# Attention and MLP block on one core: other orders for the tiles of two steps of a unit, and matmul waits on TensorE's own semaphore

## The chip, the core and the metric

The kernel runs on one core of a Trainium2 chip. The core has a matrix engine (TensorE, in the profile PE, with its weight loads as PEld), VectorE (DVE), ScalarE (ACT), GpSimd (POOL) and SyncE (SP, which issues most DMAs). Each engine works through its own queue in order; engines wait for one another by semaphores. The metric is the device time of one execution in microseconds, lower is better. Matmul results go to PSUM, of which the kernel uses eight banks of 128 x 512 float32, and from which VectorE and ScalarE read them.

## What is computed

`x` has 2048 rows of 512. After a layer norm, two branches read it: an attention block with 32 heads of 16, and an MLP of width 1376 whose output goes through a SiLU. The result is `x + s * g`.

```python
x = A_x
xn = _layernorm(x, axis=-1)
qkv = (xn @ wqkv).reshape(B, S, 3, H, Dh).transpose(2, 0, 3, 1, 4)
q, k, v = qkv[0], qkv[1], qkv[2]
p = softmax(einsum("bhqd,bhkd->bhqk", q, k) * Dh ** -0.5)
s = einsum("bhqk,bhkd->bhqd", p, v).transpose(0, 2, 1, 3).reshape(B, S, D) @ wo
h = gelu(xn @ w1 + b1)
g = silu(h @ w2 + b2)
return x + s * g
```

## The kernel before

**Stages.** Layer norm and the first projections come first (0 to 52 us), then the *dense stage* (52 to 474 us) with the remaining projections and the MLP, then the *attention stage* (to 1492 us), then the output projection of the tokens, which ends the kernel. Operands of the dense products are split into a high and a low part, so that each product is three matmuls (high by high, high by low, low by high).

**Dense stage and its row halves.** In the dense stage TensorE's array is used as two halves of 64 rows, a = 0 and a = 1, which work at the same time. `run` (L614) takes two lists of matmuls, one for each half, and issues them in turn; `fill` (L563) puts matmuls of the attention scores between them. A sum over 512 inputs is thus made partly on one half and partly on the other, in the same PSUM bank. Where a half goes on with a sum that the other half wrote last, that earlier write must be over. `mm` (L583) keeps the books for this: `writer` has the half and the number of the last matmul on each sum, and `prog["seen"]` the number of the newest matmul that is known to be over. Where the number is newer, the matmul waits for a marker. `mark` (L600) makes one: a copy of one element into `junk`, on ScalarE (or VectorE) that waits for the newest matmul so far; the later matmul then waits for the copy. Markers are put into the work ahead of need, by `down` (L645, after the fourth pair of matmuls, or two on VectorE in the last but one call) and `quad` (L702). There are 92 on ScalarE and two on VectorE. Matmuls of scores move `prog["seen"]` on as well, since they wait for VectorE, which waited for earlier ones (`taken`, L577).

**Attention stage.** A unit is four heads and 512 queries (`NU` = 32 units); a unit has 16 steps, one for each block of 128 keys. Step n belongs to unit `ua` and has the number `ka` in it, `divmod(n, 16)`. A step is written out as a string of letters (`ORDER`, L40, worked through at L970):

- T (`t_one`, L732): the scores of one head with the keys on the partitions, 128 x 512, into one of four banks; ScalarE takes the exponential from there (L741). The first two T of a step use half a = 1 of the array, the last two a = 0.
- S, X, Y (`s_op`, L209): the scores of a later unit with the queries on the partitions, needed for the maximum of the softmax; VectorE reduces each tile of 512 columns to its maximum (L189). An S is a whole tile: the first of a step uses half a = 0, the second a = 1. X and Y together are one tile: X its first 256 columns on half 0, Y its other 256 on half 1, in one bank; ahead of Y a NOP on TensorE waits until X is over (L225). One reduction follows Y.
- V (`pv_step`, L798): the exponentials of the step before times the values, for four heads, on the whole array, summed over a unit's 16 steps in one bank. When the last is done, which is the V in step ka = 0 of the next unit, VectorE copies the sum to SBUF (L811, `os`). The next unit's first V, in step ka = 1, needs that bank.

The S, X and Y tiles take turns in three banks. `s_ring` (L90) is the queue of these: S takes the oldest and puts it back at the end at once, X takes the oldest and Y puts it back. With the usual order of a step, the first S takes the bank of the last step's first S, X that of the second S, and the second S that of the halved tile. Each must wait until VectorE has reduced what is in its bank.

The string `TSXTTSTYV` is used in nearly all steps up to n = 491, where the maxima of all units are done; from there it is `TTTTV`, with the output projection between. Other work is hung on steps with `at` (L919): after the T with the index `pos`, by default the last. In step ka = 2 these are the loads of a later unit's queries (`load_qt`, six DMAs on SP's queue) and, in four units, a GpSimd subtraction for the output weights (`wo_low`).

Of the kernel before, what the change touches and what calls it, by code (L numbers as in the profile page):

```python
# [8 lines left out]
F32 = mybir.dt.float32  # L9
F32R = mybir.dt.float32r  # L10
AF = mybir.ActivationFunctionType
# [26 lines left out]
HB = 4  # L38
W2B = 2
ORDER = {0: "TTTTV", 3: "TSXTTSTYV"}  # L40
HC = CH // 2
PAIRED = 28
KB = 3
# [5 lines left out]
def fused(ctx: ExitStack, tc: tile.TileContext, x, wqk, wv, wo, w1, b1, w2, b2, out):  # L49
    nc = tc.nc  # L50
# [17 lines left out]
    ident_r = keep.tile([P, P], F32R, name="ident_r")  # L68
# [17 lines left out]
    SYNC = mybir.DependencyInfo(mybir.DependencyClass.Sync, mybir.DependencyReason.DATA)  # L86
# [5 lines left out]
    def s_tile(held=False):  # L92
        pool = s_ring.pop(0)
        if not held:
            s_ring.append(pool)
        return pool.tile([P, CH], F32, name="ps"), pool
# [58 lines left out]
    done = {u: 0 for u in range(NU)}  # L155
# [16 lines left out]
    def at_of(job):  # L172
        u, st, p = job
        return divmod(st, NCH) if u % (NCH * KB) else divmod(st, NCH)[::-1]

    def s_mm(ps, job, a, c0, k0, w):
        u, st, p = job
        qi, ki = at_of(job)
        if u not in MX:
            MX[u] = qring.tile([P, GH, NCH, NCH, 2], F32, name="mx")  # L180
        r = slice(64 * a, 64 * a + 3 * DH)
        k0 += ki * CH
        return nc.tensor.matmul(ps[:, c0:c0 + w], QS[u][r, p, qi * P:(qi + 1) * P],  # L183
                                kts[u // NCH % KB][p][r, k0:k0 + w], start=True, stop=True).ins

    def s_max(ps, job, heads, parts):
        u, p = job[0], job[2]
        qi, ki = at_of(job)
        nc.vector.tensor_reduce(MX[u][:, 2 * p:2 * p + 2, qi, ki][:, heads, parts], ps.rearrange("p (n c) -> p n c", c=HC), axis=AX.X, op=OP.max)  # L189
        done[u] += 1  # L190
        if ended:
            s_end0(ended.pop())
        if done[u] == 64:
            ended.append(u)
        if done[NU - 1] == 64:
            s_end0(ended.pop())
# [12 lines left out]
    def s_op(op):  # L209
# [6 lines left out]
        elif op == "X":  # L216
            if not cut:
                cut[:] = [jobs.pop(0), 0]
            ps, pool = s_tile(True)
            x = s_mm(ps, cut[0], 0, 0, cut[1] * HC, HC)  # L220
            cut[2:] = [ps, pool, x]
            run_off()
        else:
            job, n, ps, pool, x = cut
            hold = nc.tensor.nop().ins  # L225
            tc.add_manual_dep(hold, x.name, SYNC, reason="row tile done")
            s_mm(ps, job, 1, HC, n * HC, HC)
            s_max(ps, job, slice(0, 2), n)
# [33 lines left out]
    prog = {}  # L262
# [42 lines left out]
    for i in range(nu):  # L305
        pairs.append(ms[2 * i:2 * i + 2])
        if (i + 1) * len(qs) // nu > i * len(qs) // nu:
            g, c = qs[i * len(qs) // nu]
            pairs.append([("q", g, c), ("q", g, c + 1)])
    parts = [(c, f, h) for c in range(NCH) for f in range(FT) for h in range(2)]  # L310
    is_m = [pair[0][0] == "m" for pair in pairs]
    plan, nd = [("first", g, i) for g in range(VQ - 1) for i in (0, 2)], 0
    for j in range(len(pairs)):
        for h in range(2):
# [9 lines left out]
            n = 2 if nd < len(parts) and parts[nd][2] and ready - nd > room else 1  # L324
            n = max(n, need - 2 * (left - 1))
            while nd < ready and n > 0:
                c, f, k = parts[nd]
# [25 lines left out]
    def w2_load(i):  # L353
        if i < len(ms):
            W2[ms[i][1:]] = w_new(w2[ms[i][2]], 2, "raw2")

    def w2_split(i):
        if i < len(ms):
            W2[ms[i][1:]] = w_split(W2[ms[i][1:]], "w2", W2B)
# [178 lines left out]
    keep_r = ctx.enter_context(tc.tile_pool(name="keep_r", bufs=1, side="right"))  # L538
# [19 lines left out]
    writer = {}  # L558
    s_when, put, row = [], [0], [0, 0]
# [22 lines left out]

    def mm(a, key, ps, lhs, rhs, first, last):  # L583
        r = slice(64 * a, 64 * a + 64)
        token = None
        if not first and writer[key][0] != a and writer[key][1] > prog["seen"]:
            if not tokens or tokens[-1][0] < writer[key][1]:
                mark()
            prog["seen"], token = next(x for x in tokens if x[0] >= writer[key][1])
        i = nc.tensor.matmul(ps, lhs[r], rhs[r], start=first, stop=last).ins  # L590
        if token is not None:
            tc.add_manual_dep(i, token, SYNC, reason="other row tile")
        prog["pe"] += 1
        row[a] += 1
        latest[0] = (prog["pe"], i.name)
        writer[key] = (a, prog["pe"])

    tokens, latest = [], [None]

    def mark(dve=False):  # L600
        if dve:
            i = nc.vector.tensor_copy(junk[:, 1:], ident_r[:1, :1].bitcast(F32)).ins
        else:
            i = nc.scalar.activation(junk[:, :1], ident_r[:1, :1].bitcast(F32), AF.Copy).ins  # L604
        tc.add_manual_dep(i, latest[0][1], SYNC, reason="row tile done")
        tokens.append((latest[0][0], i.name))

    def mark_early(n):
        if prog["seen"] < n:
            mark()  # L610

    junk = keep_r.tile([1, 2], F32, name="junk")

    def run(ops, hooks={}):  # L614
        for n, two in enumerate(zip(*ops)):
            prog["n"] += 1
            for a in range(2):
                fill(a)
                mm(a, *two[a])
            for h in hooks.get(n, []):  # L620
                h()
# [23 lines left out]
    def down(c, f, part):  # L645
        i = c * FT + f
        if f == 0 and part == 0:
            PA[c] = [ps_v.tile([P, D], F32, name="pv")] + [ps_t.tile([P, D], F32, name="pst") for t in range(3)]
        h, w = HS[c, f], W2[c, f]
        side = (part + i) % 2  # L650
        ops = [[], []]
        for a in range(2):
            for t in ((0, 1), (2, 3))[(a + side) % 2]:
                ts = slice(t * P, (t + 1) * P)
                for n, (x, y) in enumerate(((0, 0), (0, 1), (1, 0))):
                    ops[a].append(((c, t), PA[c][t], h[x][:, ts], w[y],
                                   f == 0 and part == 0 and n == 0, f == FT - 1 and part == 1 and n == 2))
        n = prog["pe"]
        if (c, f, part) == parts[-2]:
            run(ops, {2: [lambda: mark(True)], 5: [lambda: mark(True)]})  # L660
        else:
            run(ops, {3: [lambda: mark_early(n)]})
        if part == 0:
            w2_split(i + 1)
            w2_load(i + 3)
            return
        del HS[c, f], W2[c, f]
        if f == FT - 1:
            for t in (0, 2, 1, 3):
                gt = wk.tile([P, D], F32, name="gt", bufs=4)  # L670
                if c == NCH - 1:
                    nc.vector.tensor_add(gt, PA[c][t], b2_sb)  # L672
                else:
                    nc.scalar.activation(gt, PA[c][t], AF.Copy)
                rs = slice(c * CH + t * P, c * CH + (t + 1) * P)
                if c < NCH - 1:
                    chores.append((gt, rs))
                else:
                    nc.gpsimd.dma_start(g_d[rs, :], gt)
# [22 lines left out]
    def quad(n, at):  # L702
        us = first[n]
        for u, b in zip(us, BANKS[n]) if at == 0 else ():
            pool, name = {"x": (ps_x, "ps"), "m": (ps_m, "ps"), "v": (ps_v, "pv"), "t": (ps_t, "pst")}[b]
            PH[u] = pool.tile([P, CH], F32, name=name)
        for i in range(at, at + 2):
            hooks = {6: [mark]} if i in (1, 2) else {}
            if n == VQ - 2 and i in (0, 2):
                hooks[3] = [lambda: w1_split(0) if i == 0 else w1_load(1)]  # L710
            run((terms(us[i], 0, i < 2), terms(us[(i + 2) % 4], 1, i < 2)), hooks)
            if i >= 2:
                for u in (us[i - 2], us[i]):
                    v_out(u[1] * NCH + u[2], PH.pop(u))
# [83 lines left out]
    def pv_step(u, k):  # L798
# [8 lines left out]
        if k == NT - 1:  # L807
# [4 lines left out]
            else:  # L812
                nc.scalar.activation(OS[u][:, :HC], pv[:, :HC], AF.Copy)
                nc.vector.tensor_copy(OS[u][:, HC:], pv[:, HC:])

# [109 lines left out]
    def due(n):  # L925
        return min(4 * L, 4 * LEAD + max(0, 3 * n - 1))

    for u in range(NU):
        g, c = divmod(u, NCH)
# [17 lines left out]
    for t in range(NW):  # L947
        n = DONE + 2 * t
# [6 lines left out]
    for i, t in enumerate(late):  # L955
        n = L - 2 * len(late) - 1 + 2 * i
# [9 lines left out]
    for n in range(L + 1):  # L966
        ua, ka = divmod(n, 16)
        want = due(n) - due(n - 1)
        i = 0
        for op in ORDER[want] if n > 1 else ("TTTTV", "TTSTSVT")[n]:  # L970
            if op in "SXY":
                s_op(op)
            elif op == "V":
                if n:
                    pv_step(*divmod(n - 1, 16))
                for _ in range(4):
                    tick()
                flush()
            else:
                if EARLY <= 4 * n + i < 4 * L:  # L980
                    t_one(ua, ka, i % 2, 1 - i // 2)
                for f, args in todo.get((n, i), []):
                    f(*args)
                i += 1
# [54 lines left out]
```

## Time and profile before

| | |
|---|---|
| median of three runs | 1581.37 us (1580.71 to 1581.43) |
| the profiled execution | 1580.84 us, of which the span from first to last instruction is 1579.0 us |
| TensorE (PE) busy | 1572.2 us of the span |
| VectorE busy | 1396.2 us |
| ScalarE busy | 1247.6 us |
| GpSimd busy | 373.6 us |
| granted TensorE clock | 1.0 throughout |

In the timeline and the chain, a line has the start in us, the length in us, the engine, the line of the kernel, the operation, the tiles written and read, the shape, and a count where several like ones are merged. What stands in brackets is the idle time ahead of the instruction on its engine and what the profile takes for its end. A line of the waits has the engine and line that waited, what it waited for, the total in us, the number of times and the longest. A busy TensorE is not TensorE at its peak: matmuls overlap, and their ends are modelled, so that starts are the better measure. An engine's idle time costs something only where that engine is on the path that sets the end.

### The profile page before, as it was taken

To read this page: it belongs to the slowest core of one execution; us is meant where nothing else is said; L and a number is where in the kernel's file an instruction comes from. 1 tells how busy PE (TensorE), PEld (TensorE's weight loads), DVE (VectorE), ACT (ScalarE), POOL (GpSimd) and SP (SyncE) were. 2 spreads that over 40 slices of the span, in tenths; PEclk is the share of its full clock that TensorE was granted. 3 is DMA by queue.
4 is the path that set the end of the run, shared out by engine and by line. 5 is a ranking of instruction groups with operands and counts; after the bars stand their busy time and mean duration, and the time that the engine had idled before them with its cause. 6 is when DMAs were issued, how large, how long until landed. Compare 5 with 4: busy or idle time off the path is not lost.

```text
span 1579.0 us, 31736 instructions
## 1 busy us (share of the span) xinstructions
PE 1572.2 (100%) x12144; PEld 949.2 (60%) x12144; DVE 1396.2 (88%) x2292; ACT 1247.6 (79%) x2489; POOL 373.6 (24%) x394
## 2 busy tenths in 40 slices
PE   9999999999999999999999999999999999999998
PEld 8899899999994444444444444444444444444445
DVE  7599898989988999999999999999999999999734
ACT  4333443434339999999999999999999999999984
POOL 4145575766641001001000100100100000000143
PEclk9999999999999999999999999999999999999999
DMA  6626343454322114111511511421150111110252
GB/s 207 151 59 154 116 138 99 147 150 122 123 84 76 43 33 68 29 36 42 82 30 29 69 38 34 56 45 29 30 76 24 33 29 36 36 30 22 60 194 101
DMA packets 74647, 116.86 MB, mean 74 GB/s; under 512 B 23012, under 2 KB 24292, under 8 KB 73320
## 3 DMA queue, kind: packets, MB, share of 16 engines
q1 hardware_dynamic: 70748, 101.89, 24.1%
q0 software_dynamic: 3264, 12.35, 4.7%
q8 instruction: 96, 1.57, 0.5%
q10 hardware_dynamic: 484, 0.60, 0.1%
q14 instruction: 55, 0.45, 0.1%
HBM read 84.35 MB, written 25.97 MB: 70 GB/s over the span
## 4 chain that ended last, share of the span: by engine, by line
PE 98%; DVE 1%; DMA 0%; issue 0%; ACT 0%; DVEq 0%
PE pv L804 33%; PE pst L739 21%; PE ps L590 13%; PE ps L183 10%; PE pst L590 7%; PE ps L739 7%; PE ps L80 3%; PE pv L590 2%; PE ps L458 1%; PE pst L80 1%; DVE st L417 0%; PE pst L440 0%; DMA xt<-in_x 0%; PE pst L458 0%; DVE slot L75 0%; DVE xn L431 0%
## 5 line engine op out<-in xcount | busy, mean ns | idle before, releaser
L189 DVE TENSOR_REDUCE mx<-ps 128x2 f32<-128x512 f32 x2048 | 1298.3, 685 | 118.6 <-PE ps L183 33.0
L741 ACT ACTIVATE slot<-pst 128x512 f32<-128x512 f32 x1533 | 825.9, 603 | 19.9 <-PE pst L739 10.5
L804 PE MATMUL pv<-slot,vsb 128*32 128x512 f32 x4096 | 545.3, 605 | 0.0
L183 PE MATMUL ps<-kt,slot 48*128 48x512 f32 x1364 | 376.4, 366 | 0.0
L739 PE MATMUL pst<-qt,kt 50*128 50x512 f32 x1149 | 372.3, 431 | 0.6 <-DVE gt L672 0.4
L739 PEld LDWEIGHTS pst<-qt,kt 50*128 50x128 f32 x1149 | 188.6, 184 | 288.3 <-ACT slot L741 261.8
L741 ACT ACTIVATE slot<-ps 128x512 f32<-128x512 f32 x515 | 311.2, 605 | 2.7 <-PE ps L183 1.8
L183 PEld LDWEIGHTS ps<-kt,slot 48*128 48x128 f32 x1364 | 224.7, 184 | 8.2 <-DVE mx L189 5.9
L590 PE MATMUL ps<-slot,w1h 64*128 64x512 f32 x1088 | 218.0, 393 | 0.0
L183 PE MATMUL ps<-kt,qz 48*128 48x512 f32 x512 | 212.8, 416 | 0.0
L183 PE MATMUL ps<-slot,slot 48*128 48x512 f32 x598 | 165.5, 366 | 0.0
L739 PE MATMUL ps<-qt,kt 50*128 50x512 f32 x387 | 159.7, 415 | 0.0
L590 PEld LDWEIGHTS ps<-slot,w1h 64*128 64x128 f32 x1088 | 151.2, 185 | 8.2 <-ACT junk L604 2.4
L590 PE MATMUL ps<-slot,w1l 64*128 64x512 f32 x544 | 141.8, 393 | 0.0
L804 PEld LDWEIGHTS pv<-slot,vsb 128*32 128x32 f32 x4096 | 80.6, 108 | 100.0 <-issue 91.8
L377 POOL TENSOR_TENSOR hl<-hg,hh 128x512 fp32r<-128x512 f32 x76 | 96.7, 1295 | 129.6 <-ACT hh L376 97.5
L250 POOL CAST nmh<-nm 128x16 fp32r<-128x16 f32 x32 | 6.3, 196 | 480.4 <-DVE nm L247 458.0
L604 ACT ACTIVATE junk<-ident_r 1x1 f32<-1x1 f32 x92 | 18.0, 196 | 119.3 <-PE pst L590 116.1
L739 PE MATMUL pst<-qt,slot 50*128 50x512 f32 x384 | 111.2, 414 | 0.0
L183 PEld LDWEIGHTS ps<-kt,qz 48*128 48x128 f32 x512 | 93.7, 183 | 15.6
L183 PEld LDWEIGHTS ps<-slot,slot 48*128 48x128 f32 x598 | 98.3, 184 | 3.1 <-DVE mx L189 2.1
L739 PEld LDWEIGHTS ps<-qt,kt 50*128 50x128 f32 x387 | 71.1, 184 | 42.1 <-ACT slot L741 36.4
(159 smaller groups left out, 1707.2 us busy)
## 6 DMA issues: line engine op xcount, KB each, us to landing
raw<-in_w SPq DMA_DIRECT2D x88, 256.0 KB
qk_h<-hh SPq DMA_DIRECT2D x32, 256.0 KB
qk_l<-hl SPq DMA_DIRECT2D x32, 256.0 KB
qt<-qk_h SPq DMA_DIRECT2D x128, 64.0 KB
slot<-qk_h SPq DMA_DIRECT2D x92, 64.0 KB
g_d<-gt POOLq DMA_DIRECT2D x16, 256.0 KB, 3.8
qt<-qk_l SPq DMA_DIRECT2D x64, 64.0 KB
dn<-den_d SPq DMA_DIRECT2D x32, 128.0 KB
```

The source lines that it names most:

```text
L80: nc.tensor.matmul(ps, lhs[a], rhs[b], start=first and n == 0, stop=last and n == 2)
L183: return nc.tensor.matmul(ps[:, c0:c0 + w], QS[u][r, p, qi * P:(qi + 1) * P], kts[u // NCH % KB][p][r, k0:k0 + w], start=True, stop=True).ins
L189: nc.vector.tensor_reduce(MX[u][:, 2 * p:2 * p + 2, qi, ki][:, heads, parts], ps.rearrange("p (n c) -> p n c", c=HC), axis=AX.X, op=OP.max)
L250: nc.gpsimd.tensor_copy(hl[:, 0], nm)
L377: nc.gpsimd.tensor_sub(hl, raw, hh.bitcast(F32))
L458: nc.tensor.matmul(pq["q", g, c], W1[g][i][:, k * P:(k + 1) * P], (xh, xl)[j][c][:, k], start=n == 0 and k == 0, stop=n == 2 and k == KT - 1)
L590: i = nc.tensor.matmul(ps, lhs[r], rhs[r], start=first, stop=last).ins
L604: i = nc.scalar.activation(junk[:, :1], ident_r[:1, :1].bitcast(F32), AF.Copy).ins
L739: nc.tensor.matmul(ps, kts[g % KB][p][r, k * P:(k + 1) * P], QT[u][r, p, :], start=True, stop=True)
L741: nc.scalar.activation(PT[u, k][:, 2 * p + a, :], ps, AF.Exp, scale=SCALE)
L804: nc.tensor.matmul(PV[u][32 * j:32 * j + 32, :], vsb[:, k, h:h + 32], PT[u, k][:, j, :], start=(k == 0), stop=(k == NT - 1))
```

## The change

Two parts. In steps with three score tiles, from the second unit on, step ka = 0 (whose V closes the unit before) and step ka = 2 get orders of their own. In the dense stage, the markers and `junk` are gone; where a matmul must wait for the other half, a NOP on TensorE waits for the very matmul that wrote the sum last, by the semaphore that this matmul itself moves on, as the NOP ahead of Y does already. The order of the matmuls in the dense stage stays.

```diff
 ORDER = {0: "TTTTV", 3: "TSXTTSTYV"}
+AFTER = {0: "STXTTSTYV", 2: "XTSTTYSTV"}
...
     def mm(a, key, ps, lhs, rhs, first, last):
         r = slice(64 * a, 64 * a + 64)
-        token = None
         if not first and writer[key][0] != a and writer[key][1] > prog["seen"]:
-            if not tokens or tokens[-1][0] < writer[key][1]:
-                mark()
-            prog["seen"], token = next(x for x in tokens if x[0] >= writer[key][1])
+            hold = nc.tensor.nop().ins
+            tc.add_manual_dep(hold, writer[key][2], SYNC, reason="other row tile")
+            prog["seen"] = writer[key][1]
         i = nc.tensor.matmul(ps, lhs[r], rhs[r], start=first, stop=last).ins
-        if token is not None:
-            tc.add_manual_dep(i, token, SYNC, reason="other row tile")
         prog["pe"] += 1
         row[a] += 1
-        latest[0] = (prog["pe"], i.name)
-        writer[key] = (a, prog["pe"])
-
-    tokens, latest = [], [None]
-
-    def mark(dve=False):
...
-    junk = keep_r.tile([1, 2], F32, name="junk")
+        writer[key] = (a, prog["pe"], i.name)
...
-        n = prog["pe"]
-        if (c, f, part) == parts[-2]:
-            run(ops, {2: [lambda: mark(True)], 5: [lambda: mark(True)]})
-        else:
-            run(ops, {3: [lambda: mark_early(n)]})
+        run(ops)
...
-            hooks = {6: [mark]} if i in (1, 2) else {}
+            hooks = {}
...
-        for op in ORDER[want] if n > 1 else ("TTTTV", "TTSTSVT")[n]:
+        order = ORDER[want] if n > 1 else ("TTTTV", "TTSTSVT")[n]
+        if want == 3 and ua:
+            order = AFTER.get(ka, order)
+        for op in order:
```

`want` is the number of score tiles due in the step: three up to n = 491. So each of the two orders is used in 30 steps.

More of the change, by code (lines that the diff above doesn't have):

```diff
@@ L584, in mm @@
         r = slice(64 * a, 64 * a + 64)
-        token = None
         if not first and writer[key][0] != a and writer[key][1] > prog["seen"]:
-            if not tokens or tokens[-1][0] < writer[key][1]:
-                mark()
-            prog["seen"], token = next(x for x in tokens if x[0] >= writer[key][1])
+            hold = nc.tensor.nop().ins
+            tc.add_manual_dep(hold, writer[key][2], SYNC, reason="other row tile")
+            prog["seen"] = writer[key][1]
         i = nc.tensor.matmul(ps, lhs[r], rhs[r], start=first, stop=last).ins
-        if token is not None:
-            tc.add_manual_dep(i, token, SYNC, reason="other row tile")
         prog["pe"] += 1
         row[a] += 1
-        latest[0] = (prog["pe"], i.name)
-        writer[key] = (a, prog["pe"])
-    tokens, latest = [], [None]
-    def mark(dve=False):
-        if dve:
-            i = nc.vector.tensor_copy(junk[:, 1:], ident_r[:1, :1].bitcast(F32)).ins
-        else:
[L604 to L610, printed above, removed]
-    junk = keep_r.tile([1, 2], F32, name="junk")
+        writer[key] = (a, prog["pe"], i.name)
     def run(ops, hooks={}):
@@ L657, in down @@
                                    f == 0 and part == 0 and n == 0, f == FT - 1 and part == 1 and n == 2))
-        n = prog["pe"]
-        if (c, f, part) == parts[-2]:
-            run(ops, {2: [lambda: mark(True)], 5: [lambda: mark(True)]})
-        else:
-            run(ops, {3: [lambda: mark_early(n)]})
+        run(ops)
         if part == 0:
```

## The prediction

> **What bounds the kernel now.** I read the page's head first, then the chain of waits, then the busy times by stage.
>
> ```profile
> span 1579.0 us, 31736 instructions
> PE 98%; DVE 1%; DMA 0%; issue 0%; ACT 0%; DVEq 0%
> core 0: us, PE busy (x) PEld busy (x) DVE busy (x) ACT busy (x) POOL busy (x), PEclk, DMA share, GB/s
> 52.00:474.00 422.00, 422.00 (x3545) 384.58 (x3547) 372.78 (x585) 159.10 (x358) 237.36 (x208) 1.00 0.42 120
> 480.00:1492.00 1012.00, 1012.00 (x7850) 475.05 (x7850) 950.88 (x1566) 1000.02 (x1962) 75.87 (x124) 1.00 0.21 41
> ```
>
> The chain that sets the end runs through TensorE for 98% of the span. The dense stage (52 to 474 us) issues a matmul every 422.00 / 3545 = 0.119 us; the attention stage (480 to 1492 us) runs 490 steps in 1012.00 us, 2.065 us a step. There ScalarE is busy for 1000.02 us too, so it could be the bound. Whether it is, the starts of the attention-times-V matmuls (the V of the order strings, one group per step) tell:
>
> ```profile
> 837.45 1.07 PE L804 MATMUL pv<-slot,vsb 128*32 128x512 f32 x8
> 838.44 0.18 PEld L739 LDWEIGHTS ps<-qt,slot 50*128 50x128 f32 x1 [0.84 <-ACT slot L741]
> 838.45 0.50 PE L183 MATMUL ps<-kt,slot 48*128 48x512 f32 x1
> ...
> 839.48 1.06 PE L804 MATMUL pv<-slot,vsb 128*32 128x512 f32 x8
> 841.55 1.07 PE L804 MATMUL pv<-slot,vsb 128*32 128x512 f32 x8
> 843.89 1.07 PE L804 MATMUL pv<-slot,vsb 128*32 128x512 f32 x8
> 845.90 1.06 PE L804 MATMUL pv<-slot,vsb 128*32 128x512 f32 x8
> 847.96 1.06 PE L804 MATMUL pv<-slot,vsb 128*32 128x512 f32 x8
> ```
>
> The 0.84 us that a step's first weight load waits are put down to ScalarE, but the preceding V group, 1.07 us long from 837.45, covers them: the next group starts when V lets the array go, 1.00 us after V began. So TensorE's own order is the bound, and what counts is a step that is longer than its neighbours. V starts lie 2.03, 2.07, 2.34, 2.01 and 2.06 us apart. The step of 2.34 us (841.55 to 843.89) is ka = 2, the next but one after the step whose V closes a unit (ka = 0, V at 839.48). The undisturbed ka = 0 goes, after its T and S at 838.45:
>
> ```profile
> 838.55 0.19 PEld L183 LDWEIGHTS ps<-kt,slot 48*128 48x128 f32 x1
> 838.79 0.28 PE L183 MATMUL ps<-kt,slot 48*128 48x256 f32 x1
> 838.90 0.39 PE L739 MATMUL pst<-qt,slot 50*128 50x512 f32 x1
> 839.01 0.40 PE L183 MATMUL ps<-kt,slot 48*128 48x512 f32 x1
> 839.14 0.41 PE L739 MATMUL pst<-qt,slot 50*128 50x512 f32 x1
> 839.25 0.28 PE L183 MATMUL ps<-kt,slot 48*128 48x256 f32 x1
> ```
>
> (the 256 columns wide ones are X and Y). The long step recurs in every unit; the waits of the attention stage show it as 30 events:
>
> ```profile
> PEld ps L183 <- DVE mx L189: 8.1, 30, 0.3
> PEld pv L804 <- DVE os L811: 6.1, 30, 0.2
> ...
> 839.01 1.89 DVE L189 TENSOR_REDUCE mx<-ps 128x2 f32<-128x512 f32 x3 [0.16 <-PE ps L183]
> 840.82 0.68 DVE L811 COPY os<-pv 128x512 f32<-128x512 f32 x1
> 841.41 3.75 DVE L189 TENSOR_REDUCE mx<-ps 128x2 f32<-128x512 f32 x6
> ...
> 842.55 0.49 PE L739 MATMUL ps<-qt,slot 50*128 50x512 f32 x1
> 843.35 0.18 PEld L183 LDWEIGHTS ps<-kt,slot 48*128 48x128 f32 x1 [0.27 <-DVE mx L189]
> 843.35 0.49 PE L183 MATMUL ps<-kt,slot 48*128 48x512 f32 x1
> 843.35 0.49 PE L739 MATMUL pst<-qt,slot 50*128 50x512 f32 x1
> 843.68 0.28 PE L183 MATMUL ps<-kt,slot 48*128 48x256 f32 x1
> ```
>
> VectorE copies the closed unit's output at 840.82, which puts its reductions 0.59 us back (840.82 to 841.41). They follow at (1.89 - 0.69) / 2 = 0.60 us each. The third after the copy, that of the halved tile of step ka = 1, ends at 841.41 + 2 x 0.60 + 0.69 = 843.30, and its bank is the one that the second S of step ka = 2 needs: that S, due 839.01 - 838.45 = 0.56 us after the step's first T, starts 0.80 us after it, at 843.35, and T, Y and V stand behind it in TensorE's order.
>
> In the dense stage, TensorE waits for a marker on ScalarE nine times, 2.4 us in all. Two of the nine:
>
> ```profile
> PEld ps L590 <- ACT junk L604: 2.4, 9, 0.3
> ...
> 161.16 0.61 PE L590 MATMUL pst<-w2h,hl 64*128 64x512 f32 x2
> 161.41 0.20 ACT L604 ACTIVATE junk<-ident_r 1x1 f32<-1x1 f32 x1 [2.31 <-PE pst L590]
> 161.67 0.50 PE L590 MATMUL ps<-slot,w1h 64*128 64x512 f32 x1
> 162.01 0.39 PE L590 MATMUL ps<-slot,w1h 64*128 64x512 f32 x2
> ...
> 364.16 0.55 PE L590 MATMUL pst<-w2h,hl 64*128 64x512 f32 x2
> 364.44 0.50 PE L590 MATMUL ps<-slot,w1h 64*128 64x512 f32 x2
> 364.78 0.61 PE L590 MATMUL ps<-slot,w1h 64*128 64x512 f32 x2
> ```
>
> **The dense stage, part by part.** The change removes 92 markers on ScalarE and two on VectorE. The code's counters make TensorE wait for one at only 12 places; the others hold nothing up. Each of the 12 becomes a NOP on TensorE that waits for the very matmul which wrote the sum before. By the same counters that matmul lies 14 matmuls back at nine places, 24 at one, and 6 plus four T tiles at two. The markers stood for a later one, about four matmuls back, and their round trip by ScalarE came on top. Fourteen matmuls are 14 x 0.119 = 1.67 us, and one is recorded as 0.50 us long (row at 161.67): the new wait is over before it is reached. A NOP whose wait is over costs nothing on the rows: every Y already has one in front, and in an undisturbed step it follows its T as closely as the others follow each other (839.14 to 839.25 is 0.11 us, as 838.79 to 838.90 and 838.90 to 839.01 in the rows of ka = 0). The worth of a removed wait: pairs are due every 2 x 0.119 = 0.24 us. After 161.16 the second next pair was due at 161.64 and came at 162.01, 0.37 us late; after 364.16 it was due at 364.64 and came at 364.78, 0.14 us late. Nine times these are 3.3 and 1.3 us; I take 2.0 us, a little under the 2.4 us of the waits, since part of each idle stretch is the ordinary distance between loads. ScalarE's freed time (92 x 0.20 = 18 us) I cost at nothing: it is busy for 159.10 of 422.00 us, and these markers are the only wait of TensorE for it that the stage lists. If a load hidden there became late, it would be a weight split, which now reaches ScalarE's queue earlier, not later.
>
> **Step ka = 2** goes from T S X T T S T Y V to X T S T T Y S T V. Of the banks that VectorE frees, X now takes the one of the last step's first S, the first S that of the second S, and the second S, as before, that of the halved tile, free at 843.30. So the wait itself stays: S still cannot start before 843.35, and T and V are behind it. What changes is that Y no longer is. Y occupies its half of the array for 0.11 us (256 columns; 838.79 to 838.90), and V comes that much sooner: 843.89 - 0.11 = 843.78. Thirty units give 30 x 0.11 = 3.3 us. X in first place is only half as long as the T beside it, but there is slack: the first S and the next T start about 0.34 us into the step, as X does now (838.79), T and Y one full slot of 0.24 us later (838.90 to 839.14), and Y is through at 842.55 + 0.34 + 0.24 + 0.11 = 843.24, before 843.35. The other end is the stall gone wholly, 2.34 - 2.06 = 0.28 us a step, 8.4 us in all; the lower end is nothing, if S and T restart slower than the stalled rows show.
>
> **Step ka = 0** goes from T S to S T at its start. Both are issued within 0.01 us, at 838.44 and 838.45, since V holds the array until then: S first can gain 0.01 us, and T lose as much. I take nothing. The upper end: VectorE waits 0.16 us for this S (row at 839.01). If S came that much sooner, the whole row of reductions would, S of ka = 2 would start at 843.19, and the stall would be nearly gone; this is the 8.4 us again, not added to it. The query loads that ka = 2 issues after its last T keep their place on SP's queue and are needed 14 steps, some 28 us, later; the subtractions of the output weights, which fall into four of these steps, keep theirs on GpSimd's.
>
> **A rule against the change.** The load of X's weights starts at 838.55 on the array half where S has been in flight since 838.45 (until 838.95). The Trainium skill, "TensorE: Matmul & The Clock Gate", section "Part 3: Packing small matmuls — row/col tiling", says that a weight load overlaps matmuls in flight only when the row group differs. By that rule, in the new ka = 2, the first S behind X and the second S behind Y, same half each, would load only after them. This trace disagrees with the rule, by the row above; what it would make of the time is the fourth case below.
>
> **The sum.** 2.0 + 3.3 = 5.3 us off the profiled execution, whose own time is 1580.84 us (span 1579.0 and 1.84 us around it, which the change does not touch): 1575.5 us. The median of the three runs, 1581.37 us, is 0.53 us above that execution, so the prediction is 1576.1 us. A measurement of this kernel can tell about 0.2%, 3.2 us, from no change: faster is under 1578.2, slower over 1584.5.
>
> **The rivals**, all about the same median.
> 1. The stall goes wholly: 8.4 + 2.0 = 10.4 us, 1571.0 us. For it speaks that VectorE has idle time (950.88 of 1012.00 busy) and needs only an advance of 0.16 us; against it, that nothing shows S of ka = 0 starting sooner than its V lets it.
> 2. Attention gains nothing, because T and V restart no sooner: the dense 2.0 us alone, 1579.4 us, no change. For it speaks that S's wait and T behind it stay.
> 3. Slower: the stall moves on to ka = 3 and is paid there in full. The second S of ka = 2 is now reduced last, and its bank is the one that the second S of ka = 3 needs. By the rows, its reduction is the third from 841.41 + 3 x 0.60 = 843.21: it begins at 844.41 at the earliest and ends at 845.10; the S that needs it stands at 843.78 + 1.00 + 0.56 = 845.34. The spare is 0.24 us. If the reduction ends later than 845.34, S, T, Y and V wait again; a stall as long as now costs 0.28 us, against 0.11 gained: 30 x 0.17 = 5.1 us lost, 2.0 won, 1584.5 us, and above that if ka = 4 waits too.
> 4. Loads wait for the same half of the array, in the new ka = 2: the first S, behind X, would load once X's 0.11 us are through, some 0.11 us late, and S and T behind it too: 30 x 0.11 = 3.3 us given back, 1579.4 us, the same as case 2.
>
> **How the numbers follow.** My forecast (1574 to 1578) 0.50; the stall gone or nearly (1568.9 to 1574) 0.22; attention without gain 0.12; the rule of same halves 0.05; stall moved on 0.11. The range must reach from most of the second to the end of the no-gain cases: 1570.0 to 1581.5, which leaves out about 0.2. Faster by over 0.2%: 0.50 + 0.22 + a little of case 2 = 0.74; within: 0.16; slower: 0.10.
>
> **What would show it.** Right: no TensorE wait for a marker between 52 and 474 us, and that stage some 2 us shorter; in step ka = 2 the second S still starts with a VectorE wait, V about 2.23 us after its predecessor, ka = 3 at 2.01 us. The stall gone: no wait of S for VectorE in ka = 2, V after 2.06 us. Wrong: a wait of S for VectorE in ka = 3, a NOP ahead of which matmuls stand apart by more than 0.12 us, or ScalarE idle ahead of its exponentials more often than now.

## The result and the profile after

| | before | after |
|---|---|---|
| median | 1581.37 us (1580.65 to 1581.85) | 1576.74 us (1576.38 to 1576.87) |
| span of the profiled execution | 1579.0 us | 1574.9 us |

The ratio is 0.9972, with a 95% interval of 0.9962 to 0.9981: the change takes 4.6 us off. The forecast of 1576.1 us was 0.6 us too low. That it came so close is in part luck: its terms were off by more than that, in both directions, and most of what follows is about them.

First, from the page of the changed kernel, the span and the chain; then the busy times by stage (columns as before):

```profile
span 1574.9 us, 31602 instructions
PE 98%; DVE 1%; DMA 0%; issue 0%; ACT 0%; DVEq 0%
```

```profile
core 0: us, PE busy (x) PEld busy (x) DVE busy (x) ACT busy (x) POOL busy (x), PEclk, DMA share, GB/s
52.00:474.00 422.00, 422.00 (x3551) 385.54 (x3553) 372.71 (x584) 146.25 (x268) 237.44 (x209) 1.00 0.42 120
480.00:1492.00 1012.00, 1012.00 (x7869) 476.29 (x7861) 951.66 (x1567) 1002.36 (x1967) 77.24 (x127) 1.00 0.20 41
```

The chain is still TensorE's. In the dense window ScalarE is freed of 159.10 - 146.25 = 12.85 us (the prediction put 18 us, and costed them at nothing), and TensorE gets only six matmuls more into the same 422 us (3551 against 3545; some records can be missing). In the attention window ScalarE does five and TensorE nineteen instructions more: there the work runs a little faster.

The first V of the attention stage starts at 477.00 us instead of 477.77: the dense stage gave 0.8 us. From there to V number 480 the time fell from 991.76 to 988.57 us: the orders gave 3.2 us. Behind V number 491, where the old string of letters serves both kernels, nothing changed (62.75 us to the last V in both).

**Dense stage.** The waits of weight loads between 52 and 474 us in the changed kernel, all of them, and the two places that the prediction showed (TensorE's timeline; the first place has its S tiles elsewhere now):

```profile
PEld ps L268 <- issue: 1.1, 3, 0.4
PEld ps L268 <- DVE mx L190: 0.4, 1, 0.4
PEld pst L590 <- issue: 0.4, 1, 0.4
```

```profile
161.20 0.39 PE L590 MATMUL pst<-w2h,hl 64*128 64x512 f32 x1
161.20 0.39 PE L590 MATMUL pst<-w2l,hh 64*128 64x512 f32 x1
161.43 0.39 PE L590 MATMUL pst<-w2h,hl 64*128 64x512 f32 x1
161.48 0.49 PE L184 MATMUL ps<-kt,qz 48*128 48x512 f32 x1
161.66 0.78 PE L590 MATMUL ps<-slot,w1h 64*128 64x512 f32 x4
...
363.55 0.54 PE L590 MATMUL pst<-w2h,hl 64*128 64x512 f32 x2
363.78 0.54 PE L590 MATMUL ps<-slot,w1h 64*128 64x512 f32 x2
364.01 0.43 PE L184 MATMUL ps<-kt,qz 48*128 48x512 f32 x1
364.16 0.53 PE L590 MATMUL ps<-slot,w1h 64*128 64x512 f32 x2
```

No wait for a marker is left. At the first place pairs now follow at 161.20, 161.43 and 161.66 us, 0.23 us apart; at the second at 363.55, 363.78 and, with the S at 364.01 between, at 364.16.

**Attention stage.** TensorE's timeline of one unit of the changed kernel, V of ka = 15, 0, 1, 2 and 3, with step ka = 2 but for its middle two T, and below it VectorE's:

```profile
769.53 1.07 PE L781 MATMUL pv<-slot,vsb 128*32 128x512 f32 x8
770.53 0.50 PE L184 MATMUL ps<-kt,slot 48*128 48x512 f32 x1
...
771.56 1.06 PE L781 MATMUL pv<-slot,vsb 128*32 128x512 f32 x8
...
773.64 1.06 PE L781 MATMUL pv<-slot,vsb 128*32 128x512 f32 x8
774.64 0.39 PE L184 MATMUL ps<-kt,slot 48*128 48x256 f32 x1
774.64 0.50 PE L716 MATMUL pst<-qt,slot 50*128 50x512 f32 x1
774.87 0.43 PE L184 MATMUL ps<-kt,slot 48*128 48x512 f32 x1
...
775.22 0.68 PE L184 MATMUL ps<-kt,slot 48*128 48x256 f32 x2
775.40 0.49 PE L716 MATMUL pst<-qt,slot 50*128 50x512 f32 x1
775.83 1.06 PE L781 MATMUL pv<-slot,vsb 128*32 128x512 f32 x8
777.84 0.64 PE L781 MATMUL pv<-slot,vsb 128*32 128x512 f32 x4
...
771.07 1.89 DVE L190 TENSOR_REDUCE mx<-ps 128x2 f32<-128x512 f32 x3
772.87 0.68 DVE L788 COPY os<-pv 128x512 f32<-128x512 f32 x1
773.47 3.75 DVE L190 TENSOR_REDUCE mx<-ps 128x2 f32<-128x512 f32 x6
```

The row at 775.22 is Y together with the second S, which starts at 775.40, beside the last T. V lies 2.19 us behind its predecessor (773.64 to 775.83), not 2.34, and the next one 2.01 us behind that. The mean over all units of a step's length, V to V, shows where the attention stage changed (the kernels with one part each are in the experiments below):

| step | before | after | ka = 2 alone | ka = 0 alone |
|---|---|---|---|---|
| ka = 0 | 2.046 | 2.034 | 2.036 | 2.041 |
| ka = 1 | 2.058 | 2.075 | 2.066 | 2.068 |
| ka = 2 | 2.339 | 2.188 | 2.225 | 2.298 |
| ka = 3 | 2.014 | 2.057 | 2.056 | 2.020 |

So ka = 2 got 0.15 us shorter, of which ka = 1 and ka = 3 gave back 0.06. The ka = 3 mean hides two kinds of units: in most it is 2.01 to 2.03 us, in every fourth (units 4, 8, ... 28) 2.18 to 2.19.

### The profile page after: what moved, and what is told of

Read it like the earlier page. It is cut to its first block, busy times and chain, and to the rows that moved or that the text cites. A ratio compares the mean times of both kernels' runs of the same rounds, so it can differ in the third digit from the quotient of the medians.

```text
span 1574.9 us, 31602 instructions
## 1 busy us (share of the span) xinstructions
PE 1568.3 (100%) x12144; PEld 949.3 (60%) x12144; DVE 1396.7 (89%) x2290; ACT 1233.7 (78%) x2397; POOL 373.0 (24%) x394
## 4 chain that ended last, share of the span: by engine, by line
PE 98%; DVE 1%; DMA 0%; issue 0%; ACT 0%; DVEq 0%
PE pv L781 33%; PE pst L716 20%; PE ps L590 12%; PE ps L184 12%; PE pst L590 7%; PE ps L716 6%; PE ps L81 3%; PE pv L590 2%; PE ps L459 1%; PE pst L81 1%; DVE st L418 0%; DMA xt<-in_x 0%; PE pst L441 0%; PE pst L459 0%; DVE slot L76 0%; DVE xn L432 0%
## 5 line engine op out<-in xcount | busy, mean ns | idle before, releaser
L184 PE MATMUL ps<-kt,slot 48*128 48x512 f32 (+1 forms) x1364 | 377.7, 368 | 0.0
L184 PE MATMUL ps<-slot,slot 48*128 48x512 f32 (+1 forms) x598 | 165.7, 366 | 0.0
L371 ACT ACTIVATE hg<-ps,b_sb 128x512 f32<-128x512 f32 x44 | 27.9, 685 | 130.8 <-PE ps L590 113.3
```

The source lines that it names most:

```text
L371: nc.scalar.activation(raw, ph.pop(u), AF.Gelu_apprx_tanh, bias=b1_sb[:, u[2]:u[2] + 1])
```

## The experiments

Each kernel ran beside the kernel before on the same chip, whose medians there were 1580.87 us (e1 to e4), 1580.41 us (e5 to e9), 1580.91 us (e10 to e12) and 1580.95 us (e13). "The changed kernel" is the starting point of an edit unless it says otherwise.

**The parts, one at a time.** e1 has the new waits without the orders:

```diff
-AFTER = {0: "STXTTSTYV", 2: "XTSTTYSTV"}
+AFTER = {}
```

> The dense stage's change alone; every step keeps the order T S X T T S T Y V. Theory (the parts add up, and the dense part is worth what the two traces show at the matmul of the same number: 0.8 us by the end of that stage): 1580.6 us, and step ka = 2 at 2.34 us in every unit. Rival (the markers' removal was worth the forecast 2.0 us, and 1.2 us of it were lost at the start of the attention stage by the new orders): 1579.4 us.

Measured: 1579.94 us (1579.37 to 1580.31), ratio 0.9994 (0.9985 to 1.0003); span 1577.6 us; first V at 476.49 us; ka = 2 at 2.338 us.

e2 has the orders and keeps the markers (the kernel before, with the lines of the change that concern the orders):

```diff
+AFTER = {0: "STXTTSTYV", 2: "XTSTTYSTV"}
...
+        order = ORDER[want] if n > 1 else ("TTTTV", "TTSTSVT")[n]
+        if want == 3 and ua:
+            order = AFTER.get(ka, order)
+        for op in order:
```

> The two orders alone, markers kept in the dense stage. Theory (the parts add up): step ka = 2 at 2.19 us, 3.2 to 3.8 us less than before, 1577.6 to 1578.2 us. Rival (the orders gain only because the dense stage ends sooner): no change, 1581 us.

Measured: 1577.54 us (1576.96 to 1577.96), ratio 0.9979 (0.9970 to 0.9988); first V at 477.63 us; ka = 2 at 2.184, ka = 3 at 2.054 us.

e3 has the order of ka = 2 alone, e4 that of ka = 0 alone, both with the new waits:

```diff
-AFTER = {0: "STXTTSTYV", 2: "XTSTTYSTV"}
+AFTER = {2: "XTSTTYSTV"}
```

> The new waits and the order of ka = 2; ka = 0 keeps the usual order. Theory (Y moved out from behind the wait makes 0.11 to 0.12 us of the 0.15 us of a step; the other 0.03 us come from ka = 0, whose S starts its reductions 0.03 us sooner): ka = 2 at 2.22 us, 30 x 0.03 = 0.9 us slower than the changed kernel, 1577.6 us. Rival (ka = 0 is worth nothing, as the prediction took it): 1576.7 us, ka = 2 at 2.19 us.

Measured: 1577.55 us (1577.26 to 1577.86), ratio 0.9979 (0.9970 to 0.9988), span 1575.5 us.

```diff
-AFTER = {0: "STXTTSTYV", 2: "XTSTTYSTV"}
+AFTER = {0: "STXTTSTYV"}
```

> The new waits and the order of ka = 0; ka = 2 keeps the usual order. Theory (ka = 0 is worth 0.03 us a unit through the stall of ka = 2): ka = 2 at 2.31 us, 0.9 us less than the waits alone, 1579.7 us. Rival (worth nothing): as the waits alone, 1580.6 us, ka = 2 at 2.34 us.

Measured: 1579.17 us (1578.73 to 1579.51), ratio 0.9988 (0.9980 to 0.9997), span 1577.6 us.

Against e1, the order of ka = 2 gives 1579.94 - 1577.55 = 2.39 us and that of ka = 0 gives 0.77 us; the waits give 1580.87 - 1579.94 = 0.93 us, though e1's interval alone does not exclude nothing. Together these are 4.1 us, beside 4.6 for the whole change. In e3 the wait of the second S can be read off directly. Its weight loads, V's and VectorE's rows in ka = 2 (same unit as above):

```profile
773.64 1.06 PE L781 MATMUL pv<-slot,vsb 128*32 128x512 f32 x8
774.84 0.18 PEld L184 LDWEIGHTS ps<-kt,slot 48*128 48x128 f32 x1
775.08 0.18 PEld L184 LDWEIGHTS ps<-kt,slot 48*128 48x128 f32 x1
775.44 0.18 PEld L184 LDWEIGHTS ps<-kt,slot 48*128 48x128 f32 x1 [0.18 <-DVE mx L190]
775.87 1.06 PE L781 MATMUL pv<-slot,vsb 128*32 128x512 f32 x8
...
772.91 0.68 DVE L788 COPY os<-pv 128x512 f32<-128x512 f32 x1
773.51 3.75 DVE L190 TENSOR_REDUCE mx<-ps 128x2 f32<-128x512 f32 x6
```

The six reductions from 773.51 follow at (3.75 - 0.69) / 5 = 0.61 us. The third ends at 773.51 + 2 x 0.61 + 0.69 = 775.42, and the S that needs its bank loads at 775.44: the wait is as before, with Y (loaded at 775.08) out from behind it. V stands 2.23 us behind its predecessor, as forecast. The whole change differs from e3 by the order of ka = 0, and there the same third reduction ends 0.04 us sooner, at 773.47 + 2 x 0.61 + 0.69 = 775.38, with the S at 775.40. Both kernels have the V of ka = 15 and ka = 0 in the same places here (769.53 and 769.54, 771.56 in both), so the 0.04 us come from VectorE.

Their origin is the S that leads ka = 0. In the changed kernel it starts at 770.53 and its reduction at 771.07, 0.54 us later; before, with T in front, the S started at 838.45 and its reduction at 839.01, 0.56 us later. Over units 1 to 30 the means are 0.565 us before, 0.565 in e1 and 0.564 in e3, and 0.536 after and 0.535 in e4. With S first the reduction can start 0.03 us sooner, though S itself starts only 0.003 us sooner; at ka = 8, where T leads in all these kernels, it is 0.564 to 0.565 in all.

**The last S and T of ka = 2 exchanged.** e12:

```diff
-AFTER = {0: "STXTTSTYV", 2: "XTSTTYSTV"}
+AFTER = {0: "STXTTSTYV", 2: "XTSTTYTSV"}
```

> The changed kernel with X T S T T Y T S V in ka = 2: T too is ahead of the S that waits. Theory (S and T behind the wait run side by side on the two halves, so that T costs V nothing): ka = 2 at 2.19 us as in the changed kernel, 1576.5 us. Rival (T behind the wait costs its 0.11 us slot, as Y did): ka = 2 at 2.08 us, 3.3 us less.

Measured: 1576.86 us (1576.12 to 1577.05), ratio 0.9973 (0.9962 to 0.9983); ka = 2 at 2.184 us, the other steps within 0.01 us of the changed kernel's. The T behind the waiting S costs nothing of its own: what the order gains is Y's place ahead of the wait.

**NOPs that wait for something long over.** e7 adds 235 of them to the dense stage, each for the matmul 14 back:

```diff
+    hist = []
...
+        elif a == 0 and len(hist) > 14 and len(hist) % 12 == 0:
+            hold = nc.tensor.nop().ins
+            tc.add_manual_dep(hold, hist[-14], SYNC, reason="extra hold")
...
+        hist.append(i.name)
```

> The changed kernel with 235 more NOPs in the dense stage, each waiting for a matmul that lies 14 matmuls of the row halves back, so that the wait is long over. Theory (such a NOP costs nothing): 1576.7 us. Rival (a NOP costs some of what the markers did, which is why the dense stage gained 0.8 us and not 2.0): (2.0 - 0.8) / 12 = 0.1 us each, 24 us more, 1600 us.

Measured: 1576.31 us (1576.03 to 1576.68), ratio 0.9973 (0.9963 to 0.9983), first V at 477.25 us. In the trace 87 of the 235 are a semaphore instruction of their own on TensorE's queue, as five of the change's twelve are; the others have none there. Together they cost nothing that can be seen, so the twelve of the change cannot be what keeps the dense stage's gain below the forecast.

**The copy taken off VectorE.** The wait in ka = 2 goes back to the copy of the closed unit. e6 makes that copy on ScalarE, with the old orders:

```diff
-AFTER = {0: "STXTTSTYV", 2: "XTSTTYSTV"}
+AFTER = {}
...
-                nc.vector.tensor_copy(OS[u], pv)
+                nc.scalar.activation(OS[u], pv, AF.Copy)
```

> The new waits, the usual order in all steps, and the copy of the closed unit on ScalarE instead of VectorE. Theory (the copy on VectorE is what makes S of ka = 2 late; ScalarE, 98.8% busy, can't take 0.6 us without making T tiles of ka = 2 wait for their banks): no wait of S for VectorE in ka = 2, but one of T for ScalarE in ka = 2 or 3, about 0.3 us; 1579.5 to 1581 us, no better than the waits alone. Rival (ScalarE takes it in its slack of 0.1 us a step): ka = 2 at 2.06 us, 1579.9 - 8.4 = 1571.5 us.

Measured: 1582.45 us (1581.88 to 1582.89), ratio 1.0013 (1.0003 to 1.0022). The attention stage's waits and ScalarE's timeline in this kernel, same unit:

```profile
PEld pst L716 <- ACT slot L718: 306.1, 399, 0.8
PEld pv L781 <- ACT os L788: 7.2, 30, 0.3
```

```profile
773.30 1.09 ACT L718 ACTIVATE slot<-pst 128x512 f32<-128x512 f32 x2
774.26 0.63 ACT L788 ACTIVATE os<-pv 128x512 f32<-128x512 f32 x1
774.74 0.64 ACT L718 ACTIVATE slot<-pst 128x512 f32<-128x512 f32 x1
```

No wait of an S for VectorE is left among the stage's waits, so the copy on VectorE was the cause of that wait. But ka = 2 is no shorter: 2.387 us. The copy takes 0.48 us of ScalarE's queue (774.26 to 774.74), the exponentials behind it are late by that, and now the T that need their banks wait: 399 such waits of T on these banks, 356 in e1. Most of either number are loads of a step's first T, which V's length covers; but within ka = 2, more than 1.02 us behind the V before, T waits for ScalarE 58 times up to 1462 us (two T in each of 29 units, 0.24 us each), and not once in e1. e9, on the changed kernel, gives ScalarE 192 of the 512 columns:

```diff
+CUT = 192
...
-                nc.vector.tensor_copy(OS[u], pv)
+                nc.vector.tensor_copy(OS[u][:, CUT:], pv[:, CUT:])
+                nc.scalar.activation(OS[u][:, :CUT], pv[:, :CUT], AF.Copy)
```

> The changed kernel, with 192 of the 512 columns of the closed unit's copy on ScalarE and 320 on VectorE. Theory (VectorE's reductions come 0.19 us sooner, and S of ka = 2 has nothing to wait for; ScalarE gets 0.3 us to take into its slack): ka = 2 at 2.06 to 2.10 us, ka = 3 at 2.02 us in all units, 30 x 0.11 = 3.3 us less, 1573.4 us. Rival (ScalarE's 0.3 us return as a wait of T for its bank): 1576.7 us or more.

Measured: 1585.52 us (1585.06 to 1585.75), ratio 1.0031 (1.0020 to 1.0043); ka = 1 at 2.196 and ka = 2 at 2.384 us. From the attention stage's waits, and from the view of the line of ScalarE's part, with its durations and what ended its idle time:

```profile
PEld pv L782 <- ACT os L790: 10.2, 30, 0.4
```

```profile
L790 ACT ACTIVATE os<-pv x31: 331/331/332, 510.0 to 1514.0; 128x192 f32<-128x192 f32 x31
its engine sat idle before it (us, times) until:
  DVE os L789: 7.2, 31
```

ScalarE's part does not run beside VectorE's but after it, with ScalarE idle for 0.23 us each time, and the next unit's first V waits longer for the bank (10.2 us in all, 6.5 in the changed kernel). In ka = 2 two T of each unit wait for ScalarE, as in e6: the rival of the expectation. Whether both parts could be made to run at once was not tried.

**The seven long steps ka = 3.** In units 4, 8, ... 28 the reduction of a unit's maxima, 0.28 us on VectorE, falls to the end of ka = 1. VectorE's timeline and TensorE's, changed kernel, unit 8, ka = 2 to ka = 3:

```profile
743.00 0.28 DVE L248 TENSOR_REDUCE nm<-mx 128x16 f32<-128x128 f32 x1
743.19 1.94 DVE L190 TENSOR_REDUCE mx<-ps 128x2 f32<-128x512 f32 x3
...
743.87 0.50 PE L716 MATMUL pst<-qt,slot 50*128 50x512 f32 x1
...
744.52 0.50 PE L184 MATMUL ps<-kt,slot 48*128 48x512 f32 x1
744.86 0.27 PE L184 MATMUL ps<-kt,slot 48*128 48x256 f32 x1
745.07 0.64 PE L781 MATMUL pv<-slot,vsb 128*32 128x512 f32 x4
```

The second S of ka = 3 needs the bank of the second S of ka = 2, which is now the last to be reduced. Its reduction is the second from 743.19: 743.19 + 0.63 + 0.69 = 744.51, and the S starts at 744.52, 0.65 us into the step instead of 0.57. Y comes 0.34 us behind it instead of 0.23, and V 2.19 us after the one before. e5 issues the reductions of maxima, those of all units in this stage, behind the fourth next score tile instead of the first:

```diff
+NMLATE = 4
...
-            s_end0(ended.pop())
+            ended[0][1] -= 1
+            if ended[0][1] <= 0:
+                s_end0(ended.pop()[0])
         if done[u] == 64:
-            ended.append(u)
+            ended.append([u, 1 if "seen" in prog else NMLATE])
...
```

> The changed kernel, but the reduction that closes a unit's maxima (nm, 0.28 us on VectorE) is issued after the fourth score tile of the next unit instead of the first. Theory (in units 4, 8, ... 28 this reduction stands between the copy of the closed unit and the reduction of the second S of ka = 2, and makes the stall come again in ka = 3): ka = 3 at 2.02 us in these seven units too instead of 2.18, 7 x 0.17 = 1.2 us less than the changed kernel, 1575.5 us. Rival (in these units a new key tile begins, and that is what holds ka = 3): still 2.18 us, 1576.7 us.

Measured: 1576.65 us (1576.47 to 1577.16), ratio 0.9976 (0.9967 to 0.9986). ka = 3 is at most 2.03 us in all units, so that reduction was the cause. But ka = 4 takes 2.21 to 2.24 us in every fourth unit, where the changed kernel has that in every eighth: the loss moved on by a step.

e10 and e13 move single reductions of maxima by four steps (twelve score tiles): e5's code with NMLATE = 13 and another condition. Both also issue the loads of finished maxima (`load_mh`) of units below 28 five steps later. e10 was meant for those in ka = 1, as its expectation says; its condition picked those of ka = 6 in units 1, 5, ... 25 instead:

```diff
+            ended.append([u, 1 if "seen" in prog or (u - 10) % 3 != 2 or u > 27 else NMLATE])
```

> The changed kernel; of the reductions that close a unit's maxima, only those that fall between the copy and ka = 3 (in units 4, 8, ... 24, six of them) are issued later, by 12 score tiles, four steps. Theory (the copy and this reduction together are what VectorE can't catch up with before ka = 3 or, as the run with a short delay showed, ka = 4; four steps on, the backlog is gone): neither ka = 3 nor ka = 4 has a stall for it, 6 x 0.17 = 1.0 us less than the changed kernel, 1575.5 us where the changed one has 1576.5. Rival (0.28 us of VectorE cost a step 0.17 us wherever they are put): no change.

Measured: 1576.70 us (1576.15 to 1577.32), ratio 0.9974 (0.9964 to 0.9984). ka = 3 is unchanged, as it must be. In units 1, 9, 17 and 25, ka = 8 falls from 2.29 to 2.06 us and ka = 12 rises by 0.23 to 0.26 us: here too the loss went where the reduction went. e13 moves the ones meant:

```diff
+            ended.append([u, 1 if "seen" in prog or (u - 11) % 3 != 0 or u > 27 else NMLATE])
```

> The changed kernel with the reductions of a unit's maxima that fall at the end of step ka = 1 in units 4, 8, ... 24 (the reduction of 0.28 us ahead of the long ka = 3) issued four steps later; the maxima that fall in ka = 6 and ka = 11 stay. (The run before it, e10_max_past_backlog, moved those of ka = 6 instead of these; there a step of 2.29 us at ka = 8 of four units went to ka = 12 of the same units, while ka = 3 kept its 2.18.) Theory A: the 0.17 us of ka = 3 in those six units is paid because VectorE has that reduction while it is still behind from the copy; four steps later it is not behind, so ka = 3 falls to 2.02 in all units but 28, nothing is lost elsewhere: 6 x 0.17 = 1.0 us off the changed kernel, some 1575.6 us. Theory B: VectorE has no spare 0.28 us anywhere in the full steps, so the reduction costs as much wherever it lands: ka = 3 falls to 2.02 and a step one or two after the new place (ka = 5 to 8) rises by about as much, 1576.7 us as before.

Measured: 1577.20 us (1576.67 to 1577.64), ratio 0.9977 (0.9967 to 0.9986). The sums over units of the step lengths, against the changed kernel's:

| ka = 3 | ka = 4 | ka = 5 | ka = 6 | ka = 7 | ka = 8 |
|---|---|---|---|---|---|
| -1.00 us | -0.30 | -0.27 | +0.71 | +0.84 | +0.52 |

The 1.0 us of ka = 3 is won as theory A has it, in six units, 0.15 to 0.18 us each; and ka = 6 to 8 lose 2.1 us, against 1.6 won in ka = 3 to 5. The 1575.6 us of theory A did not come; theory B fits: at each place tried (ka = 4 in e5, ka = 12 in e10, ka = 6 to 8 here) a full step had no room for the reduction.

**S first in every step.** If S in front costs nothing, the gain of ka = 0 is to be had elsewhere too. e11:

```diff
-ORDER = {0: "TTTTV", 3: "TSXTTSTYV"}
+ORDER = {0: "TTTTV", 3: "STXTTSTYV"}
```

> The changed kernel with S ahead of the first T in every step of the usual order, not in ka = 0 alone. Theory (what ka = 0 gains is that the first matmul of the pair is through 0.03 us sooner, which VectorE uses only where its backlog later sets a stall, after the copy; TensorE's own pace does not change): first reduction of a step 0.53 us after the load of S instead of 0.56 in every step, but the same time as the changed kernel, 1576.5 us. Rival (S first costs T, or frees VectorE, in each step): 490 x 0.03 = 15 us more, or 1 to 2 us less through the other stalls.

Measured: 1583.03 us (1582.45 to 1583.13), ratio 1.0012 (1.0003 to 1.0021), 6.3 us above the changed kernel, where none was expected. The even steps between 6 and 14 take 2.086 us instead of 2.057, the odd ones 2.042 instead of 2.038. ScalarE's rows point to the reason; first the changed kernel, around the V of ka = 13 of unit 9, at 798.52 us, then e11, around its V at 800.74:

```profile
798.02 0.60 ACT L718 ACTIVATE slot<-ps 128x512 f32<-128x512 f32 x1
798.51 1.57 ACT L718 ACTIVATE slot<-pst 128x512 f32<-128x512 f32 x3
```

```profile
800.28 0.60 ACT L718 ACTIVATE slot<-ps 128x512 f32<-128x512 f32 x1
800.77 1.57 ACT L718 ACTIVATE slot<-pst 128x512 f32<-128x512 f32 x3
```

The row with one exponential is that of the step's first T: it starts 0.50 us before V in the one and 0.46 us before it in the other, and the three behind it are late with it. Over 309 plain steps, the first exponential starts 1.535 us after the V before with T in front and 1.569 us with S in front: 0.034 us later, as S's reduction was 0.03 us sooner. S first is thus an exchange of VectorE's 0.03 us for ScalarE's. In ka = 0 VectorE is about to fall behind, and the trade is good (e4); in the other steps the time says that it is not. That ScalarE's 0.03 us make up the 6.3 us is argued, not shown: only every other step pays, and why was not found out.

## Why the prediction came out

**Where ka = 2 gains was right, and its size.** "The wait itself stays" and "V comes that much sooner": e3 alone has 2.225 us against e1's 2.338, 0.113 us for the 0.11 forecast, and the S's wait is in its rows. The 2.23 us for V was for the whole change, which made it 2.19; the missing 0.04 is the next point. e12 confirms that Y, not T, is what the order frees.

**ka = 0 was costed at nothing, and is worth 0.8 us.** "S first can gain 0.01 us": S's start did gain only 0.003 us, but its reduction begins 0.03 us sooner. The step that failed is that I took the recorded start of a matmul for the whole of what its place in a pair decides. (The 838.44 us quoted there is the start of T's weight load; the matmuls of T and S are both recorded at 838.45.) The same mechanism stands in the prediction as the upper end ("if S came that much sooner"), only I looked for it in S's start. It moved 0.03 us of the 0.16, so the first rival, the stall gone, did not come.

**The dense stage was over-sized: 2.0 us, measured 0.8 to 0.9.** The step that failed is the price of a removed wait: two places stood for nine, and each was priced by how late one pair of matmuls came against an even pace. Counted instead against the same matmul of the kernel before (the mean over the fourteen matmuls behind each wait, less the mean over the fourteen ahead of it), the changed kernel gains:

| wait of the kernel before at, us | 161.67 | 195.91 | 230.15 | 274.95 | 285.29 | 319.56 | 364.43 | 398.60 | 432.85 | sum |
|---|---|---|---|---|---|---|---|---|---|---|
| gain, us | 0.17 | 0.19 | 0.19 | 0.06 | 0.13 | 0.18 | 0.08 | 0.06 | 0.08 | 1.14 |

The two places that the prediction priced at 0.37 and 0.14 us, the first and the seventh, gave 0.17 and 0.08, and the nine gave 0.13 on the mean, not 0.22. This sum repeats: 1.06 to 1.16 us in the eleven other kernels with the new waits, and 0.02 in e2, which keeps the markers. From 56 to 473 us, though, the changed kernel gains only 0.8 us on the kernel before, so 0.3 us are lost again between the nine places, in small pieces; what takes them was not found. The NOPs are excluded by e7, which gains 0.9 us over the same stretch. The first V is a poor measure of one kernel: with the same dense code it comes anywhere from 476.43 us (e10) to 477.29 (e12). Much of that spread is there when the dense stage starts: at 56 us these kernels already lie between 0.39 us ahead of the kernel before (e10) and 0.29 behind it (e9); from 56 to 473 us they gain 0.7 to 1.1 us.

**The third rival came true in part.** "The stall moves on to ka = 3": the spare of 0.24 us holds in 23 units and does not in seven, where the reduction of the maxima, 0.28 us, stands in the queue that I counted with tiles alone. It costs 7 x 0.17 = 1.2 us, which the sum lacked. That is why ka = 2 alone is worth 2.4 us and not 3.3.

**The second and the fourth rival** forecast the same time, 1579.4 us, and neither came. The fourth went by the Trainium skill, "TensorE: Matmul & The Clock Gate", section "Part 3: Packing small matmuls — row/col tiling", whose list of what overlaps has a weight load overlap matmuls in flight only when the row group differs. (Ahead of that list the same section also lets a load into the background weight buffer go ahead of matmuls in flight, so it is the "only" of the list that a row here can speak against.) Step ka = 2 cannot decide on it: the first S loads at 774.84 us in e3, and VectorE frees its bank at 773.51 + 0.61 + 0.69 = 774.81, later than X is through by that rule too (774.64 + 0.11). Elsewhere the trace stays against the list's rule, as the prediction's row at 838.55 has it.

**The sum.** Between the two profiled executions the spans differ by 4.1 us, not 5.3: 0.8 in place of 2.0 in the dense stage, 3.2 in place of 3.3 in the attention stage, and 0.1 elsewhere. In the attention stage the 1.2 us that ka = 3 takes and the 0.8 us that ka = 0 brings leave 3.3 - 1.2 + 0.8 = 2.9 us; the other 0.3 us were not traced to a place. The medians differ by 4.6 us, 0.5 more than these two executions. So the forecast came close by luck: it had 1.2 us too much in the dense stage and lacked the 1.2 us that ka = 3 takes, and against these stand the 0.8 us of ka = 0, the 0.3 us and the spread of single executions. The place and the size of the gain at Y were not luck.

## What to carry to other kernels

Where an in-order engine must wait for a bank, first move out what stands behind the wait and does not need it: here 0.11 us a unit without touching the wait. Price a removed wait at every place where it stands, and over more matmuls than one pair behind it. Before counting on spare time on an engine, list everything in its queue in those microseconds, rare instructions too: one of 0.28 us in every fourth unit took a third of the gain back, and moving it only moved the loss. When two helpers are both full (VectorE and ScalarE at 951.66 and 1002.36 of 1012.00 us), handing the work of one to the other did not cure the stall (e6: 1582.45 us), and an order that serves one of them seems to be paid by the other (e11).

## What the hardware showed unexpectedly

- Of two matmuls that go to the two halves of the array together, the one issued first is ready 0.03 us sooner for its reader, on both sides: VectorE's reduction 0.535 instead of 0.565 us after S's start, ScalarE's first exponential 1.535 instead of 1.569 us after V. Their recorded starts differ by some thousandths of a microsecond, and their recorded ends, which are modelled, do not show it.
- 235 NOPs with a wait that is long over, put into TensorE's program, cost no measurable time (1576.31 against 1576.74 us); the trace has 87 of them as an instruction.
- The copy of a whole bank takes 0.63 us on ScalarE beside 0.68 on VectorE, but of 192 columns still 0.33 us: more than half the time for three eighths of the columns.
